# Two state-space/MLP layers on one core: k and v in two loads each, thirteen identity products at the start, one more channel group turned by TensorE each way, and a new written order

## The chip, the core and the metric

The kernel runs on one core of a Trainium2 chip. A core has five engines that run their own instruction streams: TensorE (PE in the profile; its weight loads are listed apart as PEld), VectorE (DVE), ScalarE (ACT), GpSimd (POOL) and SyncE (SP). They share an on-chip memory of 128 partitions; TensorE writes to PSUM, from which VectorE or ScalarE copies the result out (an "evacuation"). SP issues nearly all DMA transfers here. The metric is the device time of one execution in microseconds (us), as the median of several runs.

## What is computed

The input x (2048 tokens of 512 channels) goes twice through a pair of blocks; all parameters are shared between the two rounds.

```python
def _A_ref(q, k, v, shift_k, ssm_k, ssm_D):        # state-space block
    k_shift = sum over t of k_pad[:, t:t + S, :] * shift_k[:, ks - 1 - t]      # 4 taps
    kv = k_shift * v
    y = irfft2(rfft2(kv_pad) * rfft2(kf_pad))[:S]  # long convolution with ssm_k, length 2 S
    y = y + kv * ssm_D
    return q * y
def _B_ref(x, w1, b1, w2, b2):                     # channel MLP, 512 -> 1376 -> 512
    y = _layernorm(x)
    h = _gelu(y @ w1 + b1)
    return h @ w2 + b2
x = A_q
x = x + _A_ref(_layernorm(x), A_k, A_v, ...)
x = x + _B_ref(_layernorm(x), B_w1, ...)
x = x + _A_ref(_layernorm(x), A_k, A_v, ...)       # same k, v, so the same y
x = x + _B_ref(_layernorm(x), B_w1, ...)
```

The convolution result y depends on k, v, ssm_k and ssm_D alone, so the kernel computes it once, and both rounds use it.

## The kernel before

The kernel has two parts. The first, up to the line `plan.write(ORDER)` (L718), computes y and begins the first MLP. The second (L722 on) is the MLP over eight groups of 4 x 128 tokens, four for each round, with its two matrix products `mm1` (L732) and `mm2` (L766).

In the first part the order of every instruction is written out by hand. The code adds named pieces to a plan; each has a function that issues its instructions and a list of pieces that it depends on. The text `ORDER` (L18) then lists all pieces: `K24.P3` is piece K24 on TensorE with PSUM buffer 3, `K24e.A` is its evacuation on ScalarE; D is VectorE, G GpSimd, S the SP queue. Each engine runs its pieces strictly in the order of that text, so a piece that has to wait holds up everything behind it on its engine. There are four PSUM buffers of 128 x 1024 fp32 (`pf`), and a product can start only when the piece that used its buffer before has been evacuated. The pieces, in the order in which the data flow:

- **lk, lv, lx0, lx, ly, lK, lW, lM, lF, lH, w1 to w4**: loads (helper `load`, L278; lK at L345). lk0 to lk3 and lv0 to lv3 bring k and v in quarters of 512 KB; lx0 the first 512 tokens of x; lK the long filter ssm_k in quarters of 512 KB, in runs of 128 bytes; lW and lM tables. lSK, lb1 and two lh bring small vectors.
- **wm0, wm1, wm2** (L409 to L416): products of the identity with itself, whose result nobody uses; 8, 1 and 1 of them, each 128 x 512.
- **bS, bSK, bB, dg**: small vectors turned into columns, and diagonal matrices of the four taps of a channel group (L423/L425).
- **kT0 to kT3** (L431): k turned by TensorE, one quarter of the tokens each, 12 transposes; evacuated as 128 x 1536 bf16 (kT0e and so on).
- **kv, kvm** (L513, L521): the four taps as products with diagonal matrices, for three of the four channel groups (kv00 to kv03 for groups 0 and 1, kv20 and kv21 for group 2), and the product with v, which leaves u in place of v. The fourth group is done by GpSimd: **kg, ka, kgm** (L445 to L457).
- **s00, s01, s02** (L475, L478, L483, L253): the layernorm of the first 512 tokens; s00 sums on ScalarE (L475, L478) or runs the statistics on VectorE (L232).
- **KS, kd, K2** (L384, L377, L394): the transform of the filter: 16 KS pieces, then 16 K2 pieces with their evacuations; K2 can start only when all KS are evacuated. **sa0 to sb3**: eight copies of 512 KB from on-chip memory to on-chip memory (`arena<-arena`), which swap halves of the K2 result; sa0/sb0 need K20 to K23, and so on.
- **UcSq, UcTh** (`first_stage`, L302): for each of the channel groups c = 0 to 3, four products USq with evacuations into a buffer ZT, then two turns UTh. By the letter of `UT` (L214) group c is turned either by TensorE ("P", L334, 16 transposes and an evacuation of 128 x 2048 bf16 for each half) or by a DMA transpose issued by SP ("X", L281).
- **Xcj, Tcj, Vcj** (L548, L563, L571): per group c and quarter j of the frequencies: a product with evacuation, the product with the filter's spectrum on VectorE (T00 on GpSimd; it needs both copies saj and sbj), and the product back, with an evacuation of 128 x 1024 fp32. T33 and V33 are split in halves a and b.
- **Zcg or TAg to TDg** (`turn_all`, L614): the inverse's turn, for each group of tokens g = 0 to 3. By the letter of `ZM` (L215) channel group c is turned by a DMA transpose ("X", piece Zcg, L619) or by TensorE ("P", L607; TD for c = 3). For g = 0 the TensorE turn comes in two parts, a (one tile of 128 tokens) and b (three). If two groups have the letter P, their turns for g = 1 to 3 are one piece with an evacuation of twice the size.
- **Y** (L639): y for the tokens. **g, h, p, b** (L666/L667, L232, L248, L253): gate, residual and layernorm of the first group, in units of 1, 1 and 2 tiles (names ending in 0, 1, 2). **LT, M** (L647, L695): the normalised tiles turned, and the first MLP product with its GELU (L703).

One helper makes the evacuations of all these pieces (`evac`, L210 on ScalarE and L212 on VectorE), so their rows carry these two lines. The two letters before the change, and the products at the start:

```python
UT = "PPXX"
ZM = "XXXP"
for i, n in enumerate((8, 1, 1)):
    it = plan.add(f"wm{i}", {"P": 427 * n}, [], warm, take=["ps"])
```

Of the kernel before, what the change touches and what calls it, by code (L numbers as in the profile page):

```python
# [103 lines left out]
def kernel(ctx: ExitStack, tc: tile.TileContext, A_q, A_k, A_v, A_shift_k, A_ssm_k, A_ssm_D,  # L104
                 B_x, B_w1, B_b1, B_w2, B_b2, out):
    nc = tc.nc
    P = 128
    _, S, D = A_q.shape
# [44 lines left out]
    kn = place("kn", [P, NT, D], 96 * K)  # L153
    uv = place("uv", [P, NT, D], 112 * K)
    KC = P + 4
    CK = CT - 1
    kT = place("kT", [P, CK, NT, KC], 128 * K)
# [53 lines left out]
        else:  # L211
            nc.vector.tensor_copy(dst, src)  # L212

    UT = "PPXX"  # L214
    ZM = "XXXP"  # L215
    KSC, K2C = 440, 440
    EPS = 1e-5
    GT = 4
# [54 lines left out]
    with tc.tile_pool(name="ps", bufs=1, space=bass.MemoryType.PSUM) as ps:  # L273
        pf = [ps.tile([P, 1024], F32, name=f"p{i}") for i in range(4)]
        plan = _Plan({"ps": 4, "xb": NXB, "zt": NZT})

        def load(name, dst, src, nbytes, deps=(), eng="S", rank=0):
            return plan.add(name, {eng: 400}, deps, lambda it: nc.sync.dma_start(dst, src), dma=("copy", nbytes), rank=rank)  # L278
# [16 lines left out]
        def first_stage(name, src, cs, dst, deps, xbar, edeps):  # L295
# [45 lines left out]
        kd4 = k_d.rearrange(TOK, p=P)  # L341
        vd = v_d.rearrange(TOK, p=P)
# [2 lines left out]
        lK = [plan.add(f"lK{q // 2}{q % 2}", {"S": 450}, [], lambda it, q=q: nc.sync.dma_start(  # L345
            Kd[:, SQ * q:SQ * q + SQ, :], apf(A_ssm_k, SQ * q * P * NB, [[NB, P], [P * NB, SQ], [1, NB]])),
            dma=("small", 2 ** 21 // NK)) for q in range(NK)]
        lk = [load(f"lk{q}", kn[:, 4 * q:4 * q + 4, :], kd4[:, 4 * q:4 * q + 4, :], 2 ** 19) for q in range(4)]
        lv = [load(f"lv{q}", uv[:, 4 * q:4 * q + 4, :], vd[:, 4 * q:4 * q + 4, :], 2 ** 19) for q in range(4)]
        lF = load("lF", Ft[:], F_h.ap().bitcast(BF16), 2 ** 17)  # L350
        lS = [load("lSK", SKr, apf(A_shift_k, 0, [[D * KS, 1], [1, D * KS]]), 2 ** 13),
              load("lb1", b1r[:, 0:F], apf(B_b1, 0, [[F, 1], [1, F]]), 2 ** 13)]
# [14 lines left out]
        lW = load("lW", Wt[:], W_h.ap().bitcast(BF16), 2 ** 20)  # L367
        lH = load("lH", GPt[:], GP_h.ap().bitcast(BF16), 2 ** 16)
# [3 lines left out]
        for c in range(16):  # L372
            if c % (16 // NK) == 0:
                q = c * NK // 16
# [34 lines left out]
        def warm(it):  # L409
            o = view(pf[it["slot"]["ps"]], [2, 512])  # L410
            for i in range(it["n"]):
                nc.tensor.matmul(o[:, i % 2, :].rearrange("p (r c) -> p r c", c=P), IDt[:], IDw, start=True, stop=True)
        for i, n in enumerate((8, 1, 1)):
            it = plan.add(f"wm{i}", {"P": 427 * n}, [], warm, take=["ps"])
            it["n"] = n
            it["free"] = [(it, "ps")]  # L416
        kTp, kTe, dg = [], [], []
# [9 lines left out]
        for q in range(4):  # L427
            def mms(o, q=q):
                for i in range(4):
                    for ct in range(CK):  # L430
                        nc.tensor.transpose(o[:, i, ct, :], kn[:, 4 * q + i, ct * P:ct * P + P], IDt[:])  # L431
            pe, ev = mm_evac(f"kT{q}", 1250, [lk[q]], mms, [4, CK, P], lambda q=q:
                             kT[:, :, 4 * q:4 * q + 4, 2:2 + P].rearrange("p ct i c -> p i ct c"), True)
            kTp.append(pe)
            kTe.append(ev)
# [69 lines left out]
        def taps(name, ccs, nts, deps):  # L505
            n = len(ccs)

            def mms(o):
                for i, nt in enumerate(nts):
                    for j, cc in enumerate(ccs):  # L510
                        for t in range(KS):
                            w = kT[:, cc, nt - t, 2:2 + P] if nt >= t else kT[:, cc, nt - t + NT, 1:1 + P]
                            nc.tensor.matmul(o[:, i, j, :], w, DG[:, cc, t, :], start=t == 0, stop=t == KS - 1)  # L513
            pe = plan.add("kv" + name, {"P": 1800}, deps + [dg[cc] for cc in ccs],
                          lambda it: mms(view(pf[it["slot"]["ps"]], [len(nts), n, P])), take=["ps"])
            kvp.append(pe)
            lo, hi = nts[0], nts[-1] + 1

            def mul(it):
                us = uv[:, lo:hi, ccs[0] * P:(ccs[0] + n) * P].rearrange("p i (j c) -> p i j c", c=P)  # L520
                nc.vector.tensor_tensor(us, view(pf[pe["slot"]["ps"]], [len(nts), n, P]), us, ALU.mult)  # L521
            return plan.add("kvm" + name, {"D": 1150}, [pe] + lv[lo // 4:(hi + 3) // 4], mul, free=[(pe, "ps")])
        um01 = [taps(f"0{q}", (0, 1), range(4 * q, 4 * q + 4), [kTe[q], kTe[q - 1]]) for q in range(4)]
        um2 = [taps(f"2{o}", (2,), range(8 * o, 8 * o + 8), [kTe[2 * o], kTe[2 * o + 1], kTe[2 * o - 1]]) for o in range(2)]
        for cc in range(4):
# [321 lines left out]
```

## Time and profile before

| | us |
|---|---|
| median of 3 runs | 249.76 |
| the runs | 249.66, 251.34, 249.76 |
| the profiled execution: its time | 251.48 |
| the profiled execution: its span, first to last instruction | 249.7 |
| TensorE busy | 235.2 (94%) |
| VectorE busy | 168.2 (67%) |
| ScalarE busy | 141.9 (57%) |
| GpSimd busy | 58.6 (23%) |
| first product of `mm2`, that is, the end of the first part | 103.98 |

In the rows of the profile, "PE p L431 x36" is 36 matmuls of line 431 that write PSUM buffer p; an entry in square brackets is the idle time of that engine just before, and what ended it. Busy times of matmuls overlap a little, since each runs on while the next one starts. The view of windows gives the busy time of each engine in a stretch of the span. A profiled execution's own time is its span and what lies around it, here 1.78 us; it stands 1.72 us above the median of the three runs and 0.14 us above the highest of them.

### The profile page before, as it was taken

The numbers are of one execution on the slowest core, as the hardware profiler recorded it, in microseconds if no ns is written. First come the engines' busy times: TensorE is split into PE (matmuls) and PEld (weight loads), VectorE is DVE, ScalarE is ACT, GpSimd is POOL, SyncE is SP. The second block draws the span as 40 slices with busy tenths as digits, with TensorE's granted clock in tenths as the row PEclk, the third lists the DMA queues.
The fourth block names the chain that finished last, engine by engine and source line by source line (L and its number), as shares of the span: only waits on it lengthen the run. The fifth ranks groups of instructions, "written<-read, shape, count | busy, mean of one in ns | idle before, by whom it ended". The sixth has DMA issues, their size and how long they took to land.

```text
span 249.7 us, 4841 instructions
## 1 busy us (share of the span) xinstructions
PE 235.2 (94%) x1954; PEld 142.3 (57%) x1965; DVE 168.2 (67%) x319; ACT 141.9 (57%) x211; POOL 58.6 (23%) x51
## 2 busy tenths in 40 slices
PE   6699999998798889999999999999999999999994
PEld 2699884797787568644444444444444444444443
DVE  0337699996999887879879897966966862022022
ACT  2489799799898789905605604704704803803700
POOL 4079999923000031110111111010010110000000
PEclk9999999999999999999999999999999999999999
DMA  6999992999998999140400404004015015011001
GB/s 176 345 326 172 205 416 92 213 372 214 245 258 180 259 212 255 35 84 4 75 10 0 85 3 84 0 0 87 1 42 126 3 43 126 0 40 47 1 25 59
DMA packets 61169, 30.70 MB, mean 123 GB/s; under 512 B 53107, under 2 KB 56920, under 8 KB 60762
## 3 DMA queue, kind: packets, MB, share of 16 engines
q1 hardware_dynamic: 61138, 30.39, 49.4%
q8 instruction: 15, 0.25, 0.4%
q14 instruction: 8, 0.07, 0.1%
q10 hardware_dynamic: 8, 0.00, 0.0%
HBM read 15.18 MB, written 2.10 MB: 69 GB/s over the span
## 4 chain that ended last, share of the span: by engine, by line
PE 63%; DVE 3%; issue 0%; ACT 0%
PE po L766 30%; PE ph L732 27%; PE p L695 4%; PE p L639 1%; DVE arena L666 1%; DVE arena L667 1%; PE p L607 1%; DVE lstm L232 1%; PE p L647 0%; DVE arena L253 0%; ACT arena L210 0%; DVE arena L771 0%; DVE lmvm L236 0%; DVE lrsm L242 0%
## 5 line engine op out<-in xcount | busy, mean ns | idle before, releaser
L734 ACT ACTIVATE arena<-ph,B 128x512 bf16<-128x512 f32 (+1 forms) x77 | 52.9, 687 | 78.6 <-PE ph L732 78.6
L766 PE MATMUL po<-arena 128*128 128x512 bf16 (+2 forms) x356 | 77.1, 373 | 0.4
L732 PE MATMUL ph<-arena 128*128 128x512 bf16 (+1 forms) x308 | 67.6, 379 | 0.0
L766 PEld LDWEIGHTS <-arena 128*128 128x128 bf16 (+1 forms) x363 | 35.4, 98 | 40.7
L771 DVE TENSOR_TENSOR arena<-po,arena 128x512 bf16<-128x512 f32 (+1 forms) x33 | 21.6, 672 | 44.9 <-PE po L766 44.9
L732 PEld LDWEIGHTS <-arena 128*128 128x128 bf16 (+1 forms) x308 | 30.8, 100 | 35.9
L210 ACT ACTIVATE arena<-p 128x1024 bf16<-128x1024 f32 (+7 forms) x41 | 38.9, 1026 | 7.4 <-PE p L431 4.0
L248 POOL TENSOR_TENSOR lrsm<-lrsm,mhalf 128x4 f32<-128x4 f32 (+2 forms) x10 | 9.3, 927 | 81.7 <-DVE lrsm L242 81.7
L210 ACT ACTIVATE ZT<-p 128x1024 bf16<-128x1024 f32 (+1 forms) x22 | 21.8, 1017 | 2.8 <-PE p L302 1.8
L232 DVE BATCH_NORM_STATS2 lstm<-arena 128x6 f32<-128x512 bf16 x32 | 20.0, 681 | 0.2
L571 PE MATMUL p<-arena 128*128 128x128 bf16 x256 | 16.6, 219 | 3.0 <-DVE arena L563 1.5
L563 DVE TENSOR_TENSOR arena<-xb,arena 128x2048 bf16<-128x2048 bf16 (+1 forms) x16 | 17.5, 1151 | 2.3 <-DMA arena<-arena 2.2
L248 POOL TENSOR_TENSOR lrsg<-lrsg,mhalf 128x4 f32<-128x4 f32 x8 | 8.1, 1010 | 44.9 <-DVE lrsg L245 44.9
L212 DVE CAST arena<-p 128x1024 bf16<-128x1024 f32 (+1 forms) x18 | 17.3, 1012 | 0.8 <-PE p L378 0.7
L232 DVE BATCH_NORM_STATS2 lstg<-arena 128x6 f32<-128x512 bf16 x28 | 17.2, 677 | 0.0
L571 PEld LDWEIGHTS <-arena 128*128 128x128 bf16 x256 | 14.7, 98 | 4.3 <-DVE arena L563 3.3
L445 POOL TENSOR_TENSOR arena<-arena,SK 128x2048 bf16<-128x2048 bf16 (+3 forms) x4 | 15.0, 3755 | 8.5 <-PE p L431 8.3
L253 DVE TENSOR_SCALAR arena<-arena,lmvg,lrsg 128x512 bf16<-128x512 bf16 x32 | 11.0, 408 | 7.9 <-POOL lrsg L248 7.9
L253 DVE TENSOR_SCALAR arena<-arena,lmvm,lrsm 128x512 bf16<-128x512 bf16 x32 | 11.5, 416 | 3.1 <-POOL lrsm L248 3.1
L210 ACT ACTIVATE xb<-p 128x1024 bf16<-128x1024 f32 x12 | 12.2, 1071 | 1.0 <-PE p L548 1.0
L452 POOL TENSOR_TENSOR arena<-arena 128x2048 bf16<-128x2048 bf16 x3 | 12.2, 4064 | 0.2
L521 DVE TENSOR_TENSOR arena<-p,arena 128x1024 bf16<-128x1024 f32 x6 | 7.2, 1221 | 6.5 <-PE p L513 5.8
(80 smaller groups left out, 233.8 us busy)
## 6 DMA issues: line engine op xcount, KB each, us to landing
arena<-arena SPq DMA_DIRECT2D x8, 512.0 KB, 4.8
arena<-in_A_k_dram SPq DMA_DIRECT2D x4, 512.0 KB, 7.9
arena<-in_A_v_dram SPq DMA_DIRECT2D x4, 512.0 KB, 6.1
arena<-in_A_ssm_k_dram SPq DMA_DIRECT2D x4, 512.0 KB, 8.3
arena<-tabM SPq DMA_DIRECT2D x1, 2048.0 KB, 10.7
out_dram<-arena SPq DMA_DIRECT2D x15, 128.0 KB, 1.7
arena<-in_A_q_dram SPq DMA_DIRECT2D x1, 1536.0 KB
arena<-in_B_w_dram SPq DMA_DIRECT2D x1, 1376.0 KB
```

The lines of the kernel that those rows point to most:

```text
L210: nc.scalar.activation(dst, src, AF.Copy)
L212: nc.vector.tensor_copy(dst, src)
L232: nc.vector.bn_stats(self.st[:, i, 0, :], x_t[:, GT * g + i, :] if src is None else src[:, i, :])
L248: nc.gpsimd.tensor_tensor(self.rs[:, a:b], self.rs[:, a:b], mhalf[:, a:b], ALU.pow)
L253: nc.vector.tensor_scalar(out=dst[:, i, :], in0=xs, scalar1=self.mv[:, i, 0:1], scalar2=self.rs[:, i:i + 1], op0=ALU.subtract, op1=ALU.mult)
L445: nc.gpsimd.tensor_tensor(m[:, t:NT, :], kn[:, 0:NT - t, c3], sk(t, NT - t), ALU.mult)
L563: eng.tensor_tensor(kk, x2, kk, ALU.mult)
L571: nc.tensor.matmul(o[:, i, :], spec[:, cc, ka + i, :], Mt[:, ka + i, r, :], start=r == 0, stop=r == 1)
L732: nc.tensor.matmul(o.rearrange("p (i t) -> p i t", t=P), W1t[:, ct, ft * P:ft * P + m], lt[:, a:b, ct, :], start=ct == 0, stop=ct == CT - 1)
L734: nc.scalar.activation(hT[0:m, ft, a * P:b * P], o, AF.Gelu_apprx_tanh, bias=B1[0:m, ft:ft + 1])
L766: nc.tensor.matmul(po[:, a:b], hT[0:m, ft, i * P:(i + 1) * P], W2t[0:m, ft, a:b], start=ft == 0, stop=ft == FT - 1)
L771: nc.vector.tensor_tensor(xs, po[:, a:b], xs, ALU.add)
```

## The change

The loads of k and v become two of 1 MB each in place of four of 512 KB. The first piece of identity products has 13 products in place of 8. The third letters of `UT` and of `ZM` become P: the turn of u's group 2 (U2T0, U2T1) and that of the inverse's group 2 are made by TensorE in place of DMA transposes. With that the pieces Z20 to Z23 go, TC0a and TC0b come, and TD1 to TD3 become TC1 to TC3, which turn groups 2 and 3 together (16 transposes, evacuation of 128 x 2048 bf16). All pieces stand in a new order, some on another engine.

```diff
-    UT = "PPXX"
-    ZM = "XXXP"
+    UT = "PPPX"
+    ZM = "XXPP"
...
-        lk = [load(f"lk{q}", kn[:, 4 * q:4 * q + 4, :], kd4[:, 4 * q:4 * q + 4, :], 2 ** 19) for q in range(4)]
-        lv = [load(f"lv{q}", uv[:, 4 * q:4 * q + 4, :], vd[:, 4 * q:4 * q + 4, :], 2 ** 19) for q in range(4)]
+        lk = [load(f"lk{q}", kn[:, 8 * q:8 * q + 8, :], kd4[:, 8 * q:8 * q + 8, :], 2 ** 20) for q in range(2)]
+        lv = [load(f"lv{o}", uv[:, 8 * o:8 * o + 8, :], vd[:, 8 * o:8 * o + 8, :], 2 ** 20) for o in range(2)]
...
-        for i, n in enumerate((8, 1, 1)):
-            it = plan.add(f"wm{i}", {"P": 427 * n}, [], warm, take=["ps"])
+        for i, (n, c) in enumerate(((13, 11), (1, 1), (1, 1))):
+            it = plan.add(f"wm{i}", {"P": 427 * c}, [], warm, take=["ps"])
...
-            pe, ev = mm_evac(f"kT{q}", 1250, [lk[q]], mms, [4, CK, P], lambda q=q:
+            pe, ev = mm_evac(f"kT{q}", 1250, [lk[q // 2]], mms, [4, CK, P], lambda q=q:
...
-            return plan.add("kvm" + name, {"D": 1150}, [pe] + lv[lo // 4:(hi + 3) // 4], mul, free=[(pe, "ps")])
+            return plan.add("kvm" + name, {"D": 1150}, [pe, lv[lo // 8]], mul, free=[(pe, "ps")])
```

The new order, engine by engine, as far as the prediction speaks of it ("..." where pieces are left out):

```
SP before  lk2 lSK lk1 lk0 lk3 lb1 lF lh1 lx0 lh113 lv0 lv1 lv3 lv2 lK10 lK01 lK11 lK00 lW lM sb2 sa2 lH sb1 U2T0
           sa0 sb0 sa3 sa1 sb3 U2T1 U3T0 lx U3T1 ly Z10 Z00 Z11 Z20 Z01 Z21 w1 w3 Z12 Z22 Z02 Z13 Z03 Z23 w2 w4
SP after   lk0 lSK lk1 lb1 lh113 lh1 lv0 lF lK01 lK10 lv1 lH lx0 lK00 lK11 lW lM sa0 sb0 sb2 sa2 sa3 sb3 sb1 sa1
           U3T0 lx U3T1 ly Z01 Z00 Z10 Z02 Z12 w3 w4 Z11 w1 Z13 Z03 w2
PE before  wm0 bS bSK kT1 kT2 kT0 bB kT3 kv02 ... KS00 U2S2 U0S1 K211 ... V33b V33a TD0a TD2 Y00 TD0b TD1 Y01 TD3 Y02
           Y12 LT0 wm2 Y10 LT1 M0b M0a M1b LT2 M1a Y20 M2a Y22 M2b M2c Y32 Y30
PE after   wm0 bS kT0 bSK kT1 bB kT3 kT2 kv01 kv00 kv20 kd2 U0S0 wm2 KS31 ... KS71 KS61 U0S2 U2S1 U1S2 K21 ... V33b V33a
           TC0a TC0b TD0a TD0b TC1 Y01 Y02 TC2 Y00 Y12 Y10 TC3 LT1 Y20 M1b M1a LT0 Y22 LT2 M0a M0b M2b M2a M2c Y32 Y30
DVE before dg2 dg1 kT1e kT0e kvm20 kvm00 kvm02 kvm21 kvm03 kd4e kvm01 ...
DVE after  bSe kT0e bBe dg0 kT3e dg2 kvm01 kvm00 kd2e kvm20 U1S0e KS20e kvm21 s00 kvm03 kvm02 KS51e kd6e KS00e KS70e
           KS71e U0S2e U1S2e K23e K29e K210e K27e U1S3e K214e kgm U0T0e U0T1e U2S3e U1T0e T02 U2T0e U1T1e U2T1e X12e
           T10 X13e T11 T01 T12 T13 T22 T03 T30 T20 X32e T21 T23 T32 T31 T33b T33a V21e V31e TC0ae TC0be s02 Y01e g01
           h01 g02 b01 g00 h02 h00 b02 b00 LG1 LT2e
ACT after  dg1 bSKe kT1e kT2e ... U2S1e K21e K22e K20e K26e K28e K211e K24e K215e K212e K25e K213e U3S0e ... V33be V33ae
           TD0ae TD0be TC1e Y02e TC2e Y00e Y10e Y12e LT1e TC3e Y20e M1be LT0e M1ae M0ae M0be M2be M2ae M2ce Y32e Y22e Y30e
POOL after kg0 kg1 ka1 kg2 s01 ka2 kg3 ka3 T00 p01 p02 p00
```

So s00 moves from ScalarE to VectorE, kgm from GpSimd to VectorE, and of the K2 evacuations VectorE makes 5 in place of 8.

2 lines of the change are left out of this document (1 added, 1 removed).

## The prediction

> **What bounds the kernel now.** I read the chain of work that ended last first, in order of time, and then a table of windows cut where the first part changes its work: the start of the tap products (13.77), the first K2 product (37.42), the end of V33a's evacuation (81.50), the first product of `mm2` (103.98).
>
> ```profile
> 90.36 3.13 PE p L695 x56
> ...
> 103.98 9.51 PE po L766 x44
> ```
> ```profile
> core 0: us, PE busy (x) PEld busy (x) DVE busy (x) ACT busy (x) POOL busy (x), PEclk, DMA share, GB/s
> 0.00:13.77 13.77, 9.77 (x81) 6.57 (x81) 3.31 (x10) 5.05 (x10) 2.68 (x16) 1.00 0.83 274
> 13.77:37.42 23.65, 23.08 (x487) 21.56 (x485) 16.20 (x18) 21.12 (x33) 22.81 (x13) 1.00 1.04 273
> 37.42:81.50 44.08, 39.66 (x516) 32.52 (x517) 41.18 (x39) 40.70 (x43) 16.26 (x5) 1.00 0.97 224
> 81.50:103.98 22.48, 20.43 (x211) 15.60 (x215) 19.49 (x47) 19.80 (x47) 3.75 (x5) 1.00 0.87 209
> 103.98:249.70 145.72, 142.25 (x664) 66.04 (x669) 88.04 (x209) 55.23 (x80) 13.09 (x13) 1.00 0.18 40
> ```
>
> From 103.98 on the chain is TensorE without a gap; the change touches nothing there, so 145.72 stays. The rest has four stages: the load (13.77), the taps, where TensorE is busy 23.08 of 23.65, the middle, where VectorE (41.18 of 44.08) and ScalarE (40.70) are both nearly full and TensorE is not, and the tail, where TensorE has 20.43 of 22.48. An edit has to be priced by the engine that is full in its stage.
>
> **The load stage: two loads, thirteen products.** TensorE in order of time, and line 412 by itself (shortest, median and longest in ns):
>
> ```profile
> 2.07 3.59 PE L412 MATMUL p<-IDt 128*128 128x512 bf16 x8 [2.07 <-POOL mhalf L185]
> ```
> ```profile
> 8.52 4.02 PE L431 MATMUL p<-IDt,arena 128*128 128x128 bf16 x36 [1.93 <-DMA arena<-in_A_k_dram]
> 12.48 0.45 PE L365 MATMUL p<-one,arena 1*128 1x1 bf16 x11
> 12.86 1.07 PE L431 MATMUL p<-IDt,arena 128*128 128x128 bf16 x12
> 13.77 7.31 PE L513 MATMUL p<-DG,arena 128*128 128x128 bf16 x128
> ```
> ```profile
> L412 PE MATMUL p<-IDt x10: 379/634/635, 2.1 to 87.6; 128*128 128x512 bf16 x10
> ```
>
> TensorE is slow at first: 36 transposes take 4.02 (0.11 each), while 128 tap products of the same size take 7.31 (0.057). Identity products take 634 ns at the start and 379 later. The column of the granted clock says 1.00 throughout, so this is another slowing, and activity ends it: the 4.5 us from 2.07 to 6.6 (the products and the small bS and bSK) did not suffice, 4.7 us of transposes (8.52 to about 13.2, within the twelve of 12.86) did. Thirteen products at the slow spacing of 3.59/8 = 0.45 last 5.8 us, to 7.9, and are over the higher bound. So I take kT at full speed: 12 transposes in 0.7.
>
> [...]
>
> ```profile
> arena<-in_A_k_dram SPq DMA_DIRECT2D x2, 512.0 KB, 8.4
> ```
>
> kT0 needs all of lk0, 1 MB. Before, the second 512 KB ended the wait at 8.52, with the same bytes up to it: lk0 lands near 8.3. kT0, bSK, kT1 run to 9.9. lk1 ends with the bytes of the last quarter, which (row above, quarters three and four) was issued at 2.5 and landed 8.4 later: 10.9. An earlier lk0 gains nothing, since lk1 decides. kT3 and kT2 end at 12.3, so kv01 starts there, not at 13.77: **-1.5** (0.2 if the pace stays slow). The longer wm0, 2.2 us more, and bS behind it lie in the wait for k, which ends at 8.3; each us by which k came before 7.9 would be lost to them, up to where lk1 decides.
>
> **The taps.** TensorE is full here. Three more first-stage pieces (U0S2, U2S1, U1S2) stand before K21, and wm2's product: 3 x 4 x 0.11 + 0.2 = 1.5 us more. K2 so starts at 37.42 - 1.5 + 1.5 = 37.4. Walking the order piece by piece on TensorE with those durations gives 36.3; I take 37.0 (**-0.4**). Two covers must hold. kvm01 needs lv0, near 14.5 by the bytes ahead of it (3.3 MB at the rates below), and kv01 ends at 14.1. And s00 on VectorE needs lx0, which now stands behind two quarters of lK and lv1:
>
> ```profile
> 12.23 13.88 SPq L345 DMA_DIRECT2D arena<-in_A_ssm_k_dram x4
> ```
> ```profile
> arena<-in_A_q_dram SPq DMA_DIRECT2D x1, 512.0 KB, 7.7
> ```
> ```profile
> 10.00:15.00 5.00, 5.00 (x70) 4.79 (x69) 1.92 (x2) 2.66 (x3) 0.95 (x1) 1.00 1.01 345
> 20.00:25.00 5.00, 5.00 (x82) 4.84 (x80) 4.09 (x5) 4.45 (x9) 4.67 (x8) 1.00 1.13 179
> ```
> ```profile
> L232 DVE BATCH_NORM_STATS2 lstg<-arena 128x6 f32<-128x512 bf16 x4 | 2.5, 674 | 0.0
> ```
>
> Whole rows move at 345 GB/s, lK at 179. The 6.07 MB up to lx0 (5.0 whole, 1.05 of lK) take some 15 + 6 us after the first bytes at 2, plus 2 to land: 25. Bounds: issued at 12.5 and landing 7.7 later, 20.2; or each lK issue 3.47 (13.88/4) counted from 12.23 as before, then lv1 and lx0, 28.7. I take 25, nearest to the rate. s00 then holds VectorE to 28.1 (4 x 0.67 and the sums behind them), kvm03 and kvm02 wait behind it (kv03 is done at 26.6), and kv02 ends at 29.1 on TensorE: the 1.5 us of delay are just covered. ScalarE loses s00, but it had 2.5 us of slack here, so that counts nothing.
>
> **The middle.** Both evacuating engines are full, so pieces are counted.
>
> ```profile
> L563 DVE TENSOR_TENSOR arena<-xb,arena 128x2048 bf16<-128x2048 bf16 x14 | 16.3, 1218 | 2.3 <-DMA arena<-arena 2.2
> L212 DVE CAST arena<-p 128x1024 bf16<-128x1024 f32 x9 | 10.4, 1215 | 0.0
> L212 DVE CAST ZT<-p 128x1024 bf16<-128x1024 f32 x4 | 4.9, 1220 | 0.1
> L212 DVE CAST xb<-p 128x1024 bf16<-128x1024 f32 x4 | 4.9, 1220 | 0.2
> L212 DVE COPY arena<-p 128x2048 bf16<-128x2048 bf16 x3 | 3.6, 1211 | 0.0
> ```
> ```profile
> L210 ACT ACTIVATE ZT<-p 128x1024 bf16<-128x1024 f32 x18 | 18.4, 1041 | 2.3 <-PE p L302 1.3 <-PE p L571 0.7
> L210 ACT ACTIVATE xb<-p 128x1024 bf16<-128x1024 f32 x12 | 12.2, 1071 | 1.0 <-PE p L548 1.0
> L210 ACT ACTIVATE arena<-p 128x1024 bf16<-128x1024 f32 x11 | 10.8, 1043 | 0.0
> L210 ACT ACTIVATE arena<-p 128x2048 bf16<-128x2048 bf16 x1 | 1.9, 1925 | 0.0
> ```
> ```profile
> 45.85 1.18 PE L334 MATMUL p<-IDt,ZT 128*128 128x128 bf16 x16
> ```
>
> VectorE before: 14 + 9 + 4 + 4 + 3 = 34 pieces of the large size, and 2.4 us of small ones: (41.18 - 2.4)/34 = 1.14 a piece. After: U0S2e, U1S2e, 5 K2, U1S3e, U2S3e, kgm, 6 turns (two of them new), 14 T, 3 X, V21e and V31e, 35 in all, and two halves of T33: 35 x 1.14 + 1.4 = 41.3, against 41.18. ScalarE before: 41 pieces, one of 1.9 and half of V33: (40.70 - 2.5)/41 = 0.93 a piece. After: U2S1e, 11 K2, 4 U3S, 13 X, 13 V and two halves: 42 x 0.93 + 1.2 = 40.3. So the two turns cost 2.3 us on VectorE, and the moves of K2 pieces to ScalarE pay for it: the work is the same, and the stage can change only by its idle time, 2.9 on VectorE. TensorE gets 2 x 1.0 for the turns (16 transposes each, 1.18 with the last one's end) and loses 1.3: 40.4, still below.
>
> Of those 2.9, 2.2 are one wait of VectorE on a copy `arena<-arena`. Why it is late stands in SP's queue:
>
> ```profile
> 44.50 4.94 SPq L281 DMA_TRANSPOSE arena<-ZT  x1
> 49.54 4.94 SPq L278 DMA_DIRECT2D arena<-arena  x5
> 54.58 7.68 SPq L281 DMA_TRANSPOSE arena<-ZT  x2
> ```
>
> U2T0 holds SP for 4.94, and five of the eight copies stand behind it. After the change no DMA transpose is ahead of the copies: sa0 goes when K20 to K23 are evacuated (about 40), the last pair after K213e (about 47), and all have landed by 56, some 4.8 after issue; T11, the first to need the last pair, comes at 59. That wait goes (-2.2). What is late next:
>
> ```profile
> 45.66 4.11 POOL L456 TENSOR_TENSOR arena<-arena 128x2048 bf16<-128x2048 bf16 x1
> ```
> ```profile
> DMA to landing us min/median/max: 7.1/7.4/7.7
> ```
>
> kgm, now on VectorE, needs GpSimd's chain, which ended at 45.66 before (the row is the old kgm) and starts 1.5 earlier, against VectorE's own arrival at 44.8; at worst 0.5. And U3T0 (second row: shortest, median and longest of the DMA transposes of L281), issued at 54.6 and landing 7.4 later, against X30 at 62.5: near enough to cost some tenths on TensorE. I take 0.5 for these: 44.08 - 2.2 + 0.5 = 42.4 (**-1.7**; bounds 41.3, VectorE without idle, and 44.6, where another wait takes the place).
>
> **The tail.** Before, TensorE turned 32 blocks; now 64:
>
> ```profile
> 81.53 0.85 PE L607 MATMUL p<-IDt,ZT 128*128 128x128 bf16 x10 [0.71 <-DVE arena L253]
> ```
> ```profile
> L210 ACT ACTIVATE arena<-p 128x1024 bf16<-128x1024 bf16 x3 | 3.1, 1045 | 0.0
> ```
>
> 32 more transposes at 0.065 (0.85 for 10, less the last one's tail) are 2.0 us: 22.4 of work in a stage of 22.48. TC0 fills the 0.7 in which TensorE waited around V33a's evacuation, Y20 and TC1 to TC3 fill the wait for the first normalised tile. But the evacuations of TC1 to TC3 grow from 1.05 to 1.93 each on ScalarE, and two of them stand ahead of LT1e. Its queue up to there, counted from V33a's evacuation: 0.5 (TD0a on TensorE) + 1.1 (TD0ae, TD0be) + 2 x 1.8 + 3 x 0.93 (Y02e, Y10e, Y12e) + 0.5 (Y00e) + 0.4 = 8.9. So M1b starts 9.1 after that point (M0b: 90.36 - 81.5 = 8.9 before). M1b and M1a last 2.5 (44 products at 0.057); then LT0 waits for b00, VectorE's last link, at 12.3, some 0.7. The rest of TensorE's work is 10.8: together 23.1, **+0.6** (bounds 22.4, no wait at all, and 24.5, where the wait before M1b grows by another 1.4). Four DMA transposes go from SP. w1, behind eight others in SP's queue, goes out near 80 for a use at 88.5; w2, now last, near 85 for `mm2`. If w1 landed later than 88.5, each us would count.
>
> **The sum.** The start's -1.5 is spent on the pieces moved ahead of K21 and is counted in the taps' -0.4; -1.7 in the middle, +0.6 in the tail: -1.5. The profiled execution's 251.48 becomes 249.98; it stood 1.72 above the median, so the median goes from 249.76 to 248.3 (span 248.2, `mm2` at 102.5).
>
> **The rivals.**
> - *The products do not raise the pace* (or ordinary runs had it already, which would also explain why the profiled one is 1.72 above the median). kT stays at 0.11, kv01 starts 1.3 later, and some 1.0 of it reaches K2: 249.3. For it: 4.5 us of activity did not suffice. Against: 5.8 is above what did. Chance 0.18. [...]
> - *Slower: lx0 is late.* s00 blocks VectorE, with kvm03, kvm02 and every evacuation behind it, and s01 on GpSimd, with ka2, kg3, ka3 and so kgm behind it. Past 25.5 each us of lateness goes into the K2 start; landing at 28.7 it gives 251.5, and it is slower than before from 27.0 on. For it: one queue, two lK in front. Against: the rate sum. 0.13.
> - *The wait is only replaced.* Something else keeps 2.9 us of VectorE idle and the tail has its upper bound: 44.6 and 24.5, so 251.9 with the taps as forecast; half of that, 250.5, is the likely size. For it: both engines so full that any slip adds up. 0.16.
> - *All idle time closes*: K2 at 36.3, middle 41.3, tail 22.4, so `mm2` starts at 100.0, 4.0 earlier: 245.8. For it: the K2 start came out at 36.3 in the walk. Against: before, no stage ran free of idle time. 0.13.
>
> **How the numbers follow.** The forecast, 248.3, has 0.40, its own range 247.0 to 249.6. With the upper half of the fast case and most of the slow ones the range is 246.0 to 251.7. One per cent (2.5 us) is about what a measurement of this kernel can tell from no change: faster than 247.3 is the fast case and a third of the forecast, 0.26; slower than 252.3 is the far end of the second and third rivals, 0.08; the rest, 0.66, lies within.
>
> **What would show it.** L431 with a median near 220 ns and kv01 (L513) at 12.3; s00 (L232) on VectorE at 25 with the six L521 rows around it; first K2 product (L394) at 37.0; no wait of L563 on `arena<-arena`; V33a's evacuation ending at 79.4; `mm2` at 102.5. The prediction is wrong if the middle stage keeps over 2 us of idle time on VectorE, or if L210 or L647 becomes the tail's longest wait.

## The result, and the profile after

The changed kernel takes 257.3 us (median of 4 runs, 257.01 to 257.76), the kernel before 250.55 (4 runs, 249.66 to 251.65): the ratio is 1.027, with a 95% interval of 1.022 to 1.032. It is slower, and outside the range that was forecast.

The view of windows of the changed kernel, cut at the same five events as in the prediction: the start of the tap products (10.71), the first K2 product (44.63), the end of V33a's evacuation (86.03), the first product of `mm2` (109.41, as the chain has it).

```profile
0.00:10.71 10.71, 8.64 (x85) 5.21 (x86) 2.37 (x8) 4.60 (x8) 2.69 (x16) 1.00 0.81 298
10.71:44.63 33.92, 27.50 (x501) 24.27 (x498) 26.34 (x28) 18.59 (x21) 25.92 (x13) 0.90 0.82 210
44.63:86.03 41.40, 39.57 (x539) 33.78 (x539) 40.81 (x37) 39.37 (x44) 8.86 (x3) 1.00 0.78 212
86.03:109.41 23.38, 22.28 (x239) 17.55 (x243) 21.48 (x53) 22.27 (x47) 3.84 (x5) 1.00 0.60 156
109.41:255.50 146.09, 142.26 (x664) 66.08 (x669) 87.88 (x206) 55.30 (x80) 13.09 (x13) 1.00 0.18 40
```

| stage, us | before | forecast | after |
|---|---|---|---|
| load | 13.77 | 12.3 | 10.71 |
| taps | 23.65 | 24.7 | 33.92 |
| middle | 44.08 | 42.4 | 41.40 |
| tail | 22.48 | 23.1 | 23.38 |
| the rest | 145.72 | 145.72 | 146.09 |

Four stages come out at or below the forecast, or within 0.4 above it. The taps alone last 9.2 longer than forecast, so they are read first. The timeline of VectorE around their start (start, length, then what; several alike stand in one row with their count):

```profile
9.56 0.74 DVE L425 TENSOR_SCALAR DG<-IDt,sF 128x128 bf16<-128x128 bf16 x4
10.24 0.96 DVE L212 COPY arena<-p 128x1536 bf16<-128x1536 bf16 x1
11.12 8.41 DVE L425 TENSOR_SCALAR DG<-IDt,sF 128x128 bf16<-128x128 bf16 x4
19.45 2.34 DVE L521 TENSOR_TENSOR arena<-p,arena 128x1024 bf16<-128x1024 f32 x2
```

Line 425 makes the diagonal matrices. dg0, at 9.56, takes 0.74 for its four. dg2, four of the same instructions, takes 8.41. The view of the tile DG (shortest, median and longest in ns):

```profile
L425 DVE TENSOR_SCALAR DG<-IDt,sF x8: 242/252/4043, 9.6 to 19.3; 128x128 bf16<-128x128 bf16 x8
```

The median is 252 ns, the longest 4043. The timeline of GpSimd and TensorE in that time:

```profile
11.00 7.93 POOL L445 TENSOR_TENSOR arena<-arena,SK 128x2048 bf16<-128x2048 bf16 x2 [3.32 <-ACT arena L210]
...
20.71 3.57 PE L513 MATMUL p<-DG,arena 128*128 128x128 bf16 x32 [6.27 <-DVE arena L521]
```

kg0's two large instructions hold GpSimd from 11.00 to 18.93. dg2 came at 11.12, 0.12 later, and ended at 19.5. The same rows one by one, from timelines of narrow windows, each of VectorE ahead of the one of GpSimd that ran beside it:

```profile
11.12 4.04 DVE L425 TENSOR_SCALAR DG<-IDt,sF 128x128 bf16<-128x128 bf16 x1
11.00 4.11 POOL L445 TENSOR_TENSOR arena<-arena,SK 128x2048 bf16<-128x2048 bf16 x1 [3.32 <-ACT arena L210]
15.08 3.91 DVE L425 TENSOR_SCALAR DG<-IDt,sF 128x128 bf16<-128x128 bf16 x1
15.06 3.87 POOL L445 TENSOR_TENSOR arena<-arena,SK 128x1920 bf16<-128x1920 bf16 x1
18.91 0.46 DVE L425 TENSOR_SCALAR DG<-IDt,sF 128x128 bf16<-128x128 bf16 x1
18.86 0.45 POOL L447 TENSOR_TENSOR arena<-kh,SK 128x128 bf16<-128x128 bf16 x1
```

Three of dg2's four instructions start just behind one of GpSimd and end about 0.05 behind its end. kvm01 and kvm00 stand behind dg2 on VectorE; kv20 on TensorE takes kv01's PSUM buffer, which kvm01 frees, and so waits 6.27. That is the largest part of the loss. The rest is in windows of 5 us (the third number from the end is the granted clock):

```profile
10.00:15.00 5.00, 4.45 (x80) 4.33 (x78) 5.00 (x4) 2.01 (x2) 4.00 (x1) 1.00 1.06 225
15.00:20.00 5.00, 0.00 (x0) 0.00 (x0) 5.00 (x5) 0.00 (x0) 4.92 (x4) 0.91 1.15 261
20.00:25.00 5.00, 4.29 (x39) 4.03 (x38) 2.40 (x4) 0.00 (x0) 4.92 (x2) 0.50 1.14 270
25.00:30.00 5.00, 5.00 (x93) 3.70 (x92) 3.10 (x3) 3.99 (x4) 2.77 (x2) 0.90 1.12 281
```

After the wait TensorE runs at half its clock for most of 5 us: kv20's 32 products take 3.57, where the same 32 later take 1.96 and before took 1.95.

One view misleads here. The chain of work that ended last puts a transfer of ssm_k ahead of dg2:

```profile
6.65 8.33 DMA arena<-in_A_ssm_k_dram
15.08 4.45 DVE DG L425 x3
19.53 1.14 DVE arena L521
20.71 3.57 PE p L513 x32
```

dg2 reads the identity and four scalars, not ssm_k. That transfer landed at 14.98, close to the end of GpSimd's first instruction at 15.11, and releasers are inferred from events that fall together. The experiments below leave the transfer in place.

### The profile page after: what moved, and what is told of

The parts are those of the page before. It is cut to its first block, busy times and chain, and to the rows that moved or that the text cites. A ratio compares the mean times of both kernels' runs of the same rounds, so it can differ in the third digit from the quotient of the medians.

```text
span 255.5 us, 4961 instructions
## 1 busy us (share of the span) xinstructions
PE 240.3 (94%) x2021; PEld 146.9 (57%) x2034; DVE 178.9 (70%) x329; ACT 140.1 (55%) x197; POOL 54.4 (21%) x49
## 4 chain that ended last, share of the span: by engine, by line
PE 73%; DVE 10%; ACT 7%; DMA 5%; issue 2%; POOL 1%; SPq 0%; ACTq 0%; DVEq 0%; POOLq 0%
PE po L766 30%; PE ph L732 26%; PE p L513 4%; DMA arena<-in_A_ssm_k_dram 3%; ACT ZT L210 3%; PE p L695 3%; DVE arena L212 3%; ACT xb L210 3%; PE p L302 2%; DMA arena<-in_A_ssm_D_dram 2%; PE p L334 2%; PE p L384 2%; DVE DG L425 2%; ACT arena L210 2%; DVE ZT L212 1%
## 5 line engine op out<-in xcount | busy, mean ns | idle before, releaser
L210 ACT ACTIVATE arena<-p 128x1024 bf16<-128x1024 f32 (+7 forms) x45 | 43.7, 1053 | 3.1 <-PE p L384 1.6
L232 DVE BATCH_NORM_STATS2 lstg<-arena 128x6 f32<-128x512 bf16 x32 | 19.7, 677 | 0.0
L513 PE MATMUL p<-DG,arena 128*128 128x128 bf16 x192 | 13.2, 234 | 6.3 <-DVE arena L521 6.3
L563 DVE TENSOR_TENSOR arena<-xb,arena 128x2048 bf16<-128x2048 bf16 (+1 forms) x16 | 17.5, 1151 | 0.1
L513 PEld LDWEIGHTS <-arena 128*128 128x128 bf16 x192 | 12.4, 106 | 6.6 <-issue 6.4
L571 PE MATMUL p<-arena 128*128 128x128 bf16 x256 | 15.3, 219 | 0.8 <-DVE arena L563 0.5
L212 DVE CAST arena<-p 128x1024 bf16<-128x1024 f32 (+2 forms) x13 | 13.1, 1039 | 3.7 <-PE p L378 2.9
L445 POOL TENSOR_TENSOR arena<-arena,SK 128x2048 bf16<-128x2048 bf16 (+3 forms) x4 | 14.9, 3744 | 3.5 <-ACT arena L210 3.3
L571 PEld LDWEIGHTS <-arena 128*128 128x128 bf16 x256 | 14.7, 98 | 1.3 <-DVE arena L563 0.7
L210 ACT ACTIVATE xb<-p 128x1024 bf16<-128x1024 f32 x13 | 12.9, 1071 | 1.1 <-PE p L548 1.1
L253 DVE TENSOR_SCALAR arena<-arena,lmvm,lrsm 128x512 bf16<-128x512 bf16 x32 | 11.5, 417 | 2.4 <-POOL lrsm L248 2.2
```

The source lines that it names most:

```text
L210: nc.scalar.activation(dst, src, AF.Copy)
L232: nc.vector.bn_stats(self.st[:, i, 0, :], x_t[:, GT * g + i, :] if src is None else src[:, i, :])
L253: nc.vector.tensor_scalar(out=dst[:, i, :], in0=xs, scalar1=self.mv[:, i, 0:1], scalar2=self.rs[:, i:i + 1], op0=ALU.subtract, op1=ALU.mult)
L563: eng.tensor_tensor(kk, x2, kk, ALU.mult)
L571: nc.tensor.matmul(o[:, i, :], spec[:, cc, ka + i, :], Mt[:, ka + i, r, :], start=r == 0, stop=r == 1)
```

## The experiments

Theory A: dg2, whose source and destination lie in the on-chip memory, stands still while GpSimd's multiply runs, and this stall, with the clock that it costs, is all of the loss. The rivals were a cause behind dg2 (kvm01's operands), and that the loss has several causes. All edits below are to the changed kernel unless it is said otherwise; several move only a word or two of the written order. Ratios are to the kernel before, run on the same chip in the same job.

| kernel | median us | ratio, 95% interval |
|---|---|---|
| e1: dg2 on ScalarE | 248.45 | 0.9944, 0.9915 to 0.9973 |
| e1 again, other chip | 248.89 | 0.9950, 0.9931 to 0.9969 |
| e2: kg0 waits for dg2 | 248.86 | 0.9957, 0.9926 to 0.9987 |
| e3: clock kept up in the wait | 255.03 | 1.0202, 1.0134 to 1.0269 |
| e5: dg2 from PSUM, beside kg0 | 248.69 | 0.9964, 0.9937 to 0.9991 |
| e10: dg2 earlier on VectorE | 249.23 | 0.9992, 0.9957 to 1.0026 |
| e4: before with 13 products | 249.02 | 0.9966, 0.9928 to 1.0005 |
| e6: e1 with 8 products | 248.06 | 0.9933, 0.9909 to 0.9956 |
| e9: e1 with four loads | 248.92 | 0.9984, 0.9958 to 1.0010 |
| e7: e1, inverse's group 2 by DMA | 253.00 | 1.0101, 1.0055 to 1.0147 |
| e8: e1, u's group 2 by DMA | 253.77 | 1.0157, 1.0130 to 1.0184 |

**e1, dg2 by ScalarE, behind kT2e.**

```diff
-kT3.P3 kT3e.D dg2.D kT1e.A ... kT2e.A kvm01.D
+kT3.P3 kT3e.D kT1e.A ... kT2e.A dg2.A kvm01.D
```

> The changed kernel with one piece moved: dg2 on ScalarE, behind kT2e, in place of VectorE. Theory A (VectorE's four dg2 instructions cannot run beside GpSimd's kg0 and kg1, which read and write the same on-chip memory): dg2 takes 1.3 us on ScalarE, kvm01 (L521) starts near 12.8 instead of 19.45, TensorE's 6.3 us wait before kv20 goes and its pace does not drop, K2 starts some 8.8 us earlier, and the time falls from 257.3 to about 249 (248.3 to 250). Theory B (the product with v waits for the load of v, and dg2 only stands in front of it): kvm01 still starts near 19.5 and the time stays at 257.

The whole loss goes, and the kernel is faster than the one before, by 0.6% (0.3 to 0.9). The windows of e1, cut at the same events:

```profile
0.00:11.00 11.00, 8.93 (x85) 5.25 (x86) 2.37 (x8) 4.60 (x8) 2.69 (x16) 1.00 0.81 294
11.00:36.10 25.10, 24.95 (x501) 22.30 (x499) 18.21 (x24) 19.61 (x25) 24.24 (x12) 1.00 1.00 250
36.10:77.70 41.60, 39.83 (x545) 34.12 (x544) 41.00 (x38) 39.83 (x44) 10.57 (x4) 1.00 0.82 232
77.70:100.56 22.86, 21.79 (x235) 17.17 (x238) 21.18 (x51) 21.79 (x46) 3.85 (x5) 1.00 0.61 156
100.56:246.70 146.14, 142.27 (x665) 66.08 (x669) 87.89 (x206) 55.31 (x80) 13.08 (x13) 1.00 0.18 40
```

The taps last 25.10 for 33.92; no other stage changes by more than 0.6. And VectorE's next row after the evacuations:

```profile
13.05 1.23 DVE L521 TENSOR_TENSOR arena<-p,arena 128x1024 bf16<-128x1024 f32 x1 [1.55 <-PE p L513]
```

kvm01 runs at 13.05 and had waited for its product alone, so v's first load was there: nothing behind dg2 was late. It also runs beside kg0 (GpSimd's L445 from 11.29 to 19.24) in its usual 1.23; one of its two operands lies in PSUM.

**e2, the same order of VectorE, but GpSimd held back until dg2 is done.** kg0's multiply gets a copy of one column of dg2's result ahead of it on GpSimd.

```diff
+            if not t:
+                nc.gpsimd.tensor_copy(wt0[:], DG[:, 2, KS - 1, 0:1])
```

> The changed kernel, VectorE's order untouched; a copy of one element of dg2's result is put ahead of kg0 on GpSimd, so that GpSimd starts its taps only when dg2 is done. Theory A: dg2 takes about 0.75 us in all instead of 8.41, kg0 starts near 12.2 instead of 11.0, kvm01 near 12.6, and the time falls to about 249 to 250 as in the run with dg2 on ScalarE (GpSimd 1.2 us later costs at most some tenths). Theory B, or dg2 slow by itself: dg2 stays at 8 us or kvm01 stays near 19.5, and the time is 257 to 258.

The timeline of VectorE, then that of GpSimd (line numbers are one to three higher here):

```profile
11.56 0.73 DVE L426 TENSOR_SCALAR DG<-IDt,sF 128x128 bf16<-128x128 bf16 x4
```
```profile
12.64 7.95 POOL L448 TENSOR_TENSOR arena<-arena,SK 128x2048 bf16<-128x2048 bf16 x2
```

dg2 stays where it was on VectorE and takes 0.73; GpSimd's start moves by 1.6, which costs 0.4 at most (248.86 against e1's 248.45 in the same job). So what stalled dg2 was GpSimd, not its place.

**e3, the wait stays, but TensorE is kept busy in it** by 24 identity products ahead of kv20.

```diff
-kv20.P0 kd2.P3 U0S0.P20 kd2e.D wm2.P1 U0S0e.A
+wm2.P1 kv20.P0 kd2.P3 U0S0.P20 kd2e.D U0S0e.A
...
-        for i, (n, c) in enumerate(((13, 11), (1, 1), (1, 1))):
+        for i, (n, c) in enumerate(((13, 11), (1, 1), (24, 24))):
```

> The changed kernel with the wait left in, and wm2 as 24 identity products (24 x 0.216 = 5.2 us) between kv00 and kv20, so that TensorE works through the wait. Theory C (an idle time of 6 us lowers TensorE's pace for the next 5 us, which costs 2.3 to 2.5 us on top of the wait): kv20 still starts near 20.7, its 32 products take 1.9 us instead of 3.57, the matmul spacing stays at 0.056 and the time falls by 2 to 2.5 us to about 255. Without theory C: kv20 as slow as before and 257.

```profile
14.66 5.34 PE L412 MATMUL p<-IDt 128*128 128x512 bf16 x24
...
21.07 1.95 PE L513 MATMUL p<-DG,arena 128*128 128x128 bf16 x32 [1.07 <-DVE arena L521]
```

kv20 starts 0.36 later than in the changed kernel but takes 1.95 for 3.57, and the time falls by 2.3 (257.3 to 255.03; the two medians are of different jobs). From the first tap product to the first K2 product the traces have 33.92 in the changed kernel, 31.31 in e3 and 25.10 in e1: of these 8.8, then, 2.6 are the clock and 6.2 the wait itself.

**e5 and e10, which part of "dg2 on VectorE" does it.** e5 keeps dg2 on VectorE and beside kg0, but reads the identity from PSUM, where an identity product (wm1, moved forward) has put it; e10 keeps everything, and puts dg2 ahead of kT3e.

```diff
-bBe.D dg0.D kT3.P3 kT3e.D dg2.D kT1e.A kT2.P2
+bBe.D dg0.D kT3.P3 kT3e.D kT1e.A kT2.P2 wm1.P1 dg2.D
...
+                    if ct == 2:
+                        nc.vector.tensor_scalar(out=dst, in0=view(pf[1], [2, 512])[:, 0, 0:P], ...)
```
```diff
-bB.P2 bBe.D dg0.D kT3.P3 kT3e.D dg2.D kT1e.A
+bB.P2 dg0.D dg2.D bBe.D kT3.P3 kT3e.D kT1e.A
```

> The changed kernel with dg2 still on VectorE and still while GpSimd runs kg0, but its source is an identity in PSUM (the product of wm1, moved ahead of kv01) instead of the one in on-chip memory. [...]

> The changed kernel with dg2 on VectorE as in the change, but straight behind dg0 and ahead of bBe and kT3e, so that it is done near 10.4, before GpSimd's kg0 starts at 11. Theory A: dg2 takes 0.75 us, kvm01 starts near 13, and the time is that of the run with dg2 on ScalarE, 248 to 249.2: it is the place in the order, not the engine, that costs 8 us. If kT3e, now 0.3 us later, delays kv00, some tenths more.

VectorE and GpSimd in e5 (L423 is the line that reads PSUM there, L447 the multiply):

```profile
11.83 1.12 DVE L423 TENSOR_SCALAR DG<-p,sF 128x128 bf16<-128x128 f32 x4
```
```profile
11.70 7.95 POOL L447 TENSOR_TENSOR arena<-arena,SK 128x2048 bf16<-128x2048 bf16 x2 [4.19 <-ACT arena L210]
```

dg2 starts 0.13 after kg0, as in the changed kernel, and takes 1.12 for four (341 ns each). Expected were 248.5 to 249.5 if a source in PSUM lets dg2 pass, and near 257 if it does not; the median is 248.69. The operation, the engine and the moment are the same; the source differs, in its place and with it in its type (fp32 for bf16). Which of these two lets dg2 pass was not separated. In e10 dg2 is done before kg0 starts at 12.05:

```profile
9.58 1.38 DVE L425 TENSOR_SCALAR DG<-IDt,sF 128x128 bf16<-128x128 bf16 x8
```

Eight in 1.38, at a median of 248 ns. So VectorE was no wrong place for dg2 either, only that moment.

**e6, e4 and e9: what the products and the two loads are worth.** e6 is e1 with eight products, e9 is e1 with k and v in four loads each in the same order of bytes, e4 is the kernel before with thirteen products.

```diff
-        for i, (n, c) in enumerate(((13, 11), (1, 1), (1, 1))):
+        for i, (n, c) in enumerate(((8, 8), (1, 1), (1, 1))):
```

> As the reference beside it (dg2 on ScalarE), but 8 identity products at the start in place of 13. If the products raise TensorE's pace before k lands: kT0 to kT2 run at 0.107 us a transpose, kv01 starts near 12.5 to 13.0 instead of 11.0 (the 48 transposes cost 2.4 us more, less the 0.9 by which kT0 can start earlier), K2 starts 1.0 to 1.5 later and the time rises by 0.7 to 1.5. If VectorE's queue hides it: no change (within 0.4).

> The changed kernel with dg2 on ScalarE once more, as the reference for the three runs beside it, each of which takes one part of the change back from it: 248.0 to 249.0, 0.3 to 0.8% below the kernel before.

> The kernel before with 13 identity products at the start in place of 8, nothing else. If the thirteen products raise TensorE's pace: the transposes of L431 take 0.22 us each from the first on, the 36 of them some 2.0 us in place of 4.0, and kv02 starts near 12.3 to 12.8 (bounded by the last quarter of k), 1.0 to 1.5 earlier; the time falls by 0 to 1.3 us, since VectorE and ScalarE bound the middle. If not: L431 stays at 0.31 and the time is unchanged.

> The changed kernel with dg2 on ScalarE, and k and v in four loads of 512 KB each again, in the same order of bytes. If two loads land earlier than four (kT3 found lk1 landed by 9.4 in the changed kernel, while the last quarter landed at 10.9 before): kT3 starts at 10.5 to 11 and kv01 1 us later, and the time rises by 0 to 0.7. If the number of loads does not matter and only what stands behind them in the queue did: kT and kv01 as with two loads (kv01 at 11.0 to 11.5) and 248.0 to 249.0.

TensorE in e6, in order of time, and then in e1:

```profile
6.08 1.46 PE L431 MATMUL p<-IDt,arena 128*128 128x128 bf16 x12
...
9.78 2.28 PE L431 MATMUL p<-IDt,arena 128*128 128x128 bf16 x24
```
```profile
7.43 0.84 PE L431 MATMUL p<-IDt,arena 128*128 128x128 bf16 x12
...
9.65 1.51 PE L431 MATMUL p<-IDt,arena 128*128 128x128 bf16 x24
```

With eight products TensorE is slow in the transposes (1.46 for 12, against 0.84) but begins them at 6.08, without waiting: k was there. With thirteen they begin at 7.43. kv01 starts at 11.90 and 11.00, and these two executions take 249.38 and 248.46: the 0.9 comes out whole at the end. Two more executions say the same: kv01 starts at 11.46 in e1 again and at 11.62 in e9, and they take 248.89 and 248.99. In all four, what follows kv01's start takes 237.4 to 237.5.

The medians do not show it: 248.06 with eight products against 248.89 with thirteen (0.9933 against 0.9950 in the same job, each interval holding the other's value). My expectation of +0.7 to +1.5 missed. But the profiled execution of e6 stands 1.3 above the median of its twelve runs. If 237.45 follows kv01 in the usual one too, kv01 starts near 10.6 there (an estimate), and no such execution was profiled. What the five products are worth in the usual execution therefore stays open.

In the kernel before, thirteen products shorten the 36 transposes from 4.02 to 2.18 and bring the first tap product (kv02 there) to 11.28, 2.5 earlier. The time changes by 0.3% with an interval that reaches 1.0005. The execution that was profiled took 252.81, the longest of its ten, so its trace does not show where the 2.5 went in the others. Four loads for two: 248.92, in a job in which e5 took 248.69 and e10 249.23; no difference shows.

**e7 and e8, each turn back to DMA** in e1's order: e7 the inverse's group 2 (Z20 to Z23 in SP's queue), e8 u's group 2.

```diff
-    ZM = "XXPP"
+    ZM = "XXXP"
```
```diff
-    UT = "PPPX"
+    UT = "PPXX"
```

> As the reference, but the inverse's group 2 turned by DMA transposes again (Z20 to Z23 back, TC0 out, TC1 to TC3 as TD1 to TD3). The forecast priced this part at +0.6 in the tail, so that taking it back should give -0.5 to -1.0: 2.0 us less on TensorE and 2.7 us less on ScalarE between V33a's evacuation and mm2, where TensorE is full. Rival: Y01 then waits for Z20, which can be issued only after V22e and V21e, near the end of the middle, and lands 4 us later; then the tail grows by 1 to 2 us and the time rises.

> As the reference, but u's group 2 turned by DMA transposes again (U2T0, U2T1 on SP behind the eight copies, ahead of U3T0). If the turn by TensorE is what frees the copies and X20: U2T0 is issued near 51 and lands near 58, U3T0 moves from 53 to about 61 and lands near 68, X20 and X30 wait for them, VectorE and ScalarE fall idle in the middle for 3 to 6 us, and the time rises by 2 to 5 us, although 2.3 us of VectorE's evacuations go. Rival: the DMA turn is hidden, the middle gets shorter by about 1 us, and so does the time.

The view of waits (in total, times, longest), first e7, then e8:

```profile
PE p L639 <- DMA arena<-ZT: 4.3, 2, 2.6
```
```profile
PE p L548 <- DMA arena<-ZT: 4.8, 1, 4.8
```

Against e1 in the same job (248.89), e8 costs 4.9 and e7 4.1 by the medians, 5.2 and 3.8 by the ratios: TensorE waits for a transposed tile, 4.8 for X20 in e8 and 4.3 for the Y products in e7. e7's waits are those of its longest run, 254.85; its six runs lie between 250.94 and 254.85. For e8 the size was expected; for e7 a gain of 0.5 to 1.0 was, and the rival held, at more than its 1 to 2. In this order each turn by TensorE is needed. It does not follow that each would gain this much in the order before, which was written for DMA.

**The kernel before, profiled again**, because its first profiled execution stood above its median.

> The kernel before, unchanged, profiled a second time: its profiled execution of 251.48 stands some 1.5 above the median of its runs (249.9), and it is open where in the span these 1.5 lie. Theory A (they lie in the load stage: TensorE's pace and the landing of k vary from run to run): if this execution takes about 249.9, the first tap product starts 1 to 2 us before 13.77, and the stages behind it last what they did (23.65, 44.1, 22.5) within some tenths. Theory B (they lie in the middle, where the copies and DMA transposes in SP's queue land early or late): the first tap product starts within 0.5 of 13.77, and the middle stage is 1 to 2 us shorter than 44.1, with less than 2.2 us of waiting of VectorE on copies. If this execution takes 251 or more, it tells nothing.

It took 250.42. Three of its windows, cut at the same events:

```profile
0.00:12.87 12.87, 8.76 (x81) 6.18 (x82) 3.29 (x10) 5.06 (x10) 2.69 (x16) 0.87 0.81 269
12.87:36.46 23.59, 23.08 (x487) 21.54 (x484) 16.17 (x19) 21.06 (x33) 22.75 (x13) 1.00 1.06 286
36.46:80.35 43.89, 39.72 (x517) 32.52 (x517) 41.24 (x39) 40.77 (x43) 16.36 (x5) 1.00 0.96 225
```

It is 1.06 faster than the execution that the prediction read, and 0.90 of that is the load stage (12.87 for 13.77), a little less than the 1 to 2 expected. The other stages repeat within 0.2, so here too the earlier start comes out whole at the end. One more execution is not a distribution, but it shows where the spread of this kernel's times can come from. No other execution of it near the median was profiled.

## Why the prediction was wrong

**The failed step: the order of VectorE in the taps, "Two covers must hold".** I listed two things that could delay the evacuations there, the landing of lv0 and of lx0, and both held. dg2, which the new order puts between kT3e and kvm01 in VectorE's queue, was given neither a price nor a place. Two rows of before show what hid it:

```profile
6.48 1.39 DVE L425 TENSOR_SCALAR DG<-IDt,sF 128x128 bf16<-128x128 bf16 x8 [6.48 <-ACT sF L210]
14.05 7.96 POOL L445 TENSOR_TENSOR arena<-arena,SK 128x2048 bf16<-128x2048 bf16 x2 [8.30 <-PE p L431]
```

Eight in 1.39, done by 7.9, while GpSimd's first multiply started at 14.05. The changed order moves dg2 later and kg0 earlier until they meet, at 11.12 and 11.00. At 0.25 each the four would have been done by 12.1, ahead of the product that kvm01 needs, which ends near 13; the meeting made them last 8.4. No rival held it either: the slow cases were slow products, late transfers and full engines, and the slower one (lx0) did not occur, since in e1 VectorE began s00 at 23.62 without waiting for lx0, against 25 forecast. The 2 us to land in that forecast are an estimate that fits lx0 in the kernel before: it was issued at 5.55, the windows there have moved the 2.85 MB up to its last byte by about 11.3, and it landed at 13.25, 7.7 after its issue.

What the traces show of the cause is that each instruction of dg2 that came just behind one of GpSimd ended just behind its end: 4.04, 3.91 and 0.46 beside GpSimd's 4.11, 3.87 and 0.45. In e5, whose source lies in PSUM, none stalled (341 to 350 ns). Why an instruction of GpSimd holds up one of VectorE was not shown.

**The load stage: the direction right, the sizes off.** Twelve transposes took 0.84, near the 0.7 assumed. The transposes (L431) have a median of 219 ns in nine profiled executions with thirteen products and of 314 in all three with eight, so the products did raise the pace, and the first rival's cause did not occur. But lk0, forecast to land at 8.3, was there by 6.08 (e6), and lk1, forecast at 10.9, by 9.36, where the last 24 transposes start without waiting. kv01 so came at 10.71 for 12.3. Since k came before 7.9, the longer product piece delayed kT0 instead of hiding, which the prediction named as the condition. The forecast let most of the start's gain go to the pieces ahead of K21; in e1 the start came 2.77 earlier (11.00 for 13.77), these pieces took 1.45 of it, and 1.32 reached K2.

**The taps otherwise.** Without the stall (e1) they last 25.10 for 24.7 forecast, and K2 starts at 36.10 for 37.0: the three pieces ahead of K21 and wm2's product cost what was counted (1.45 for 1.5).

**The middle: right.** 41.40 for 42.4. The wait of L563 on the copies is gone (idle before its rows 0.1 in this stage, 2.2 before) and nothing took its place; VectorE is busy 40.81, forecast 41.3. The two turns cost what the moved K2 pieces pay for, and e8 shows the price of the DMA turn in their place.

**The tail: right.** 23.38 (22.86 in e1) for 23.1, with TensorE's longest single wait at 0.3.

**The sum.** With the failed step out, e1 gains 1.4 on the median (0.9944 of 249.91), where 1.5 was forecast. That is closer than the steps were: up to `mm2` e1 lies 3.42 ahead of the profiled execution (100.56 for 103.98), twice the forecast, while that execution itself stood 1.5 above the median of before's runs. I carried the 1.72 over as a constant; the second profile puts 0.9 of it into the load stage, the very stage that the change shortens. So the last agreement is partly luck. The chance of 0.08 for slower was too small because every slow case was priced by transfers and by busy engines, none by two engines in each other's way.

## What to carry to other kernels

When an order is rewritten, list for each moved instruction of VectorE what GpSimd runs at its new moment; here a start 0.12 us behind GpSimd's turned four instructions of 0.25 into 8.4 and left TensorE waiting 6.27. A row whose longest instruction is many times its median (252 and 4043 ns) is the sign to look for, and the cures are cheap: another engine, an earlier place, a source in PSUM, or a short wait on the other engine, all between 0.9944 and 0.9992 of the kernel before. And read what an earlier start is worth from profiled executions, event by event, and say how far each stands from its median: in four of them here each tenth of it came out at the end, while the medians of eight and thirteen products did not differ.

## What the runs showed of the hardware

- A tensor-by-scalar of VectorE between tiles in on-chip memory took 242 to 256 ns alone and 4.04 us beside GpSimd's 128x2048 product of 4.11. VectorE instructions with a PSUM operand went on beside the same product: 1.23 for L521, 341 ns for dg2 from PSUM. Between back-to-back instructions the two engines took turns: three of VectorE (4.04, 3.91, 0.46) each ended about 0.05 behind one of GpSimd (4.11, 3.87, 0.45), and the fourth passed in 0.24.
- After 6.27 us without a product TensorE's granted clock was 0.50 from 20 to 25, which cost 2.3 to 2.6. After the wait of 1.07 in e3 no product slowed: the 192 tap products there (L513, 11.1 to 34.8) took 216 to 231 ns, against up to 311 in the changed kernel.
- The slowness of the first microseconds, which the prediction called "another slowing" because the column of the granted clock reads 1.00 there, is most likely the halved clock too. In the second execution of the kernel before, the 36 transposes have the same duration as in the first (a median of 314 ns), and there the column shows it:

```profile
L431 PE MATMUL p<-IDt,arena x48: 219/314/314, 8.1 to 12.8; 128*128 128x128 bf16 x48
```
```profile
8.00:10.00 2.00, 1.91 (x20) 1.92 (x21) 0.54 (x1) 0.00 (x0) 0.00 (x0) 0.57 1.05 366
10.00:12.00 2.00, 2.00 (x26) 1.89 (x25) 0.48 (x2) 1.26 (x1) 0.00 (x0) 0.58 1.04 335
12.00:14.00 2.00, 2.00 (x44) 1.98 (x41) 0.90 (x1) 1.31 (x3) 0.85 (x1) 1.00 0.99 390
```

  There the products were faster at their end (3.25 for eight, against 3.59), TensorE then had little to do from 5.3 to 8.1, with no product in the last 2.0 of it, and the clock went down at about 8.2. Transposes alone brought it back by 12 (0.50 from 11 to 11.5, 1.00 from 12). So a reading of 1.00 ahead of a trace's first change of clock does not say that the clock was full. In two packed traces the record of the clock begins with 1.00 and holds nothing ahead of it: it begins at 13.38 in the execution that the prediction read and at 5.48 in the changed kernel, which are the moments at which the products become faster (transposes of 291 ns on average from 12.9 to 13.4 and 238 from 13.4 to 14; identity products of 634 ns from 4 to 5 and 379 from 6 to 7). That the clock was half before is inferred from the durations, not recorded.
- The thirteen identity products from 2.07 on took 4.33 (e4) to 5.55 (e9) in different executions: the moment at which TensorE reaches its pace moves from one execution to the next.
